# Attention, soft mixture of experts and feed-forward in one kernel: the first pair without conversions, idle transposes and four fold products at the end of attention, one early chunk of w_out

## The chip, the cores and the metric

The kernel runs on one core of a Trainium2 chip. The metric is the device time of one execution in microseconds; where several runs are given, it is their median.

## What is computed

Three stages follow one another. `attn` has 4 batches of 8 heads, 576 positions and 64 dimensions; its result, with the heads side by side, is the input `x` (2304 x 512) of the mixture; the mixture's result is the input of the feed-forward part.

```python
# attention, per head
bias   = -(cumsum(max(s, 0))[i] - cumsum(max(s, 0))[j])
scores = where(causal, -1e9, q @ k.T / 8 + minimum(bias, 0))
x      = softmax(scores) @ v                       # heads side by side: 2304 x 512
# soft mixture of 8 experts with 4 slots each
logits = x @ phi                                   # 2304 x 32
d      = softmax over tokens(logits);  slot_input = d.T @ x
slot_out[e] = maximum(slot_input[e] @ w1[e], 0) @ w2[e]      # 512 -> 1024 -> 512
x      = softmax over slots(logits) @ slot_out
# feed-forward part
h = x @ w_in                                       # 512 -> 2048
g = where(h >= 1, h, where(h <= -1, 0, (h + 1)**2 / 4))
out = g @ w_out                                    # 2048 -> 512
```

`w_in` and `w_out` are 64-bit floats in memory (8 and 8 MB); the kernel reads them as pairs of 32-bit words and makes 32-bit floats of them.

## The kernel before

**Attention** goes over 16 pairs of heads. For each pair TensorE makes the scores (`s_mm`, L267), VectorE the masked minima (`maxima`, L299, recorded at L293), ScalarE the exponentials with their sums (`exps`, L328), TensorE transposes them (L338), ScalarE evacuates the transposes (`evac_p`, L353 and L361), TensorE multiplies by `v` (L369, L377), ScalarE evacuates (L383, L384), and logits (L412) and transposes of the result (L405) follow a pair later. The scores of a pair come in four groups of query blocks; group 2 is the tail of 64 queries of both heads. The bias enters the scores through a second product with the rows `ext`, which come by DMA from `part`, three bfloat16 pieces of the running sum (L222 to L229).

The order of all this is written out by hand: `PLAN` (L52) gives each step a time within its pair of 12 units, `GATE` (L59) does so for the mixture's running softmax of a batch, and the steps are sorted by time and issued. The engines work in the order of issue. All DMAs but two are issued from SP's queue, in order.

Five steps of each pair, W0 to W4, advance `convert_wi` (L581): it loads `w_in` in 32 stages of 256 KB and converts each with one operation on POOL (L601) and two on VectorE (L602, L604). Its first step only starts two stage loads (L590). Each further step issues one half of a stage's work; all of it is done after 65 steps, in the 13th pair. In the plan W1 stands behind the last exponential of group 1 (time 3.9), and M20, the minima of group 2, behind W4 (6.43). The rest of the conversion, `finish_wi` (L608), is 64 operations of VectorE while the experts run.

**The end of attention** (L645 to L677) is the last pair's logits and transposes, then the last batch's gate: `d1` (maximum over blocks), `d2` (transpose and maximum over partitions), `d3` (the maximum is broadcast, `dn` = logits minus maximum; `al4`, the factor for the older sums, as an exponential on ScalarE), `d4` (exponential of `dn`), `c0` to `c2` (the softmax over slots), `d5` (sums, L497, and products with X, L500 and L502, in `pa`), `d6` (running sums). Then the four 32-row groups are folded into one: for each of four blocks of 128 columns one product of the older sum `acc` with `fold_al` (L670) and one of the new part, copied out of PSUM, with `fold` (L671). The result divided by its total is `siT` (L675), which the experts read. `c3` transposes the slot weights into `cstack` (L542, L548, L552).

**The experts** (L691 to L782) run one after the other: `layer1` (L695, then a transpose, L702) and `layer2` (L711, then copy `os` on ScalarE, L714, a transpose, L717, and a copy to `soT`, L718). Their weights come in tiles of 512 KB, four for each `w1` and each `w2`, in the order of `LOADS` (L40). There are 38 places for a tile: 12 `pre` and 10 `post` ones that are filled during attention, 6 more `post` ones and 7 `tmp` ones that exist when the buffers of the heads are free (L649 to L652), and 3 `tmp` ones when all buffers of attention are free (L684). `load_w` (L104) issues loads from SP for as long as there is a free place; a place is given back with the last product that reads it. In the list two chunks of `w_out` (`wo`) stand ahead of the last eight tiles; `wo` may only take a `pre` place. From the third chunk on, the loads of `wo` wait behind a small DMA (`gate`, L126) that reads the last `w2` tile.

Ahead of the last expert's `layer2` the two early chunks are converted to the 32-bit parts `wh` and `wl` (`convert_wo`, L732): one operation on ScalarE (L148), three on VectorE (L150, L152, L154), a cast on ScalarE (L740) and a difference on VectorE (L742).

**The feed-forward part** does not form the mixture's output. It forms M = slot_out @ w_in (`m_part`, L797) once, stacks parts of it (`split_m`, `stack_m`), and then goes over blocks of 384 tokens and 16 blocks of the hidden dimension: `h_part` (product with `cstack`, L830, and two ScalarE activations, L832 and L833), `g_part` (L840 on VectorE, L842 on ScalarE), `l_part` (L848 on VectorE), `o_part` (27 records of products: L858 with `wh`, L859 with `wl`, L860 with `wh`). The first two token blocks alternate, so each chunk of `w_out` is used in two steps running. Chunk n's six conversion steps are spread over the loop's steps from `NWIN * n + CONV_AT` on (L788 to L791).

Of the kernel before, what the change touches and what calls it, by code (L numbers as in the profile page):

```python
# [8 lines left out]
F32 = mybir.dt.float32  # L9
# [3 lines left out]
AF = mybir.ActivationFunctionType  # L13
# [26 lines left out]
LOADS = [(_k, _q) for _k in W_ORDER for _q in range(4)]  # L40
WO_EARLY = 2
WO_SLOTS = 6
LOADS[-8:-8] = [("wo", _q) for _q in range(WO_EARLY)]
LOADS += [("wo", _q) for _q in range(WO_EARLY, 16)]
CHUNK = 256
PRE_FROM, PRE_STEP = (5, 2.4)
NWIN = 2
CONV_AT = -5
CONV_PARTS = 6
# [15 lines left out]
def attention_softmoe_ffn_kernel(  # L65
# [43 lines left out]
    def load_parts():  # L109
        while w_next[0] < len(LOADS):  # L110
            key, q = LOADS[w_next[0]]
            if key == "wo":
                slot = next((f for f in w_free if f[0] == "pre"), None) if len(wo_used) < WO_SLOTS else None
            else:
                slot = w_free[0] if w_free else None
# [4 lines left out]
            if key == "wo":  # L120
                t = t.bitcast(I32)
                wo_used.append(q)
                if q == WO_EARLY:

                    last = w_tiles[W_ORDER[-1]][3][0]
                    nc.sync.dma_start(out=gate[0:1], in_=last[0:1, 0:1])  # L126
                w_wo[q] = t, slot
                src = w_src[key][q // 4][:, 1024 * (q % 4):1024 * (q % 4) + 1024]
            else:
                w_tiles.setdefault(key, []).append((t, slot))  # L130
                src = w_src[key[0]][key[1]][:, 1024 * q:1024 * q + 1024]
# [9 lines left out]

    def convert(src, a, out):

# [3 lines left out]
        ai = a.bitcast(I32)  # L147
        A.activation(out=a, in_=hi.bitcast(F32), func=AF.Copy, scale=2.0 ** -112)  # L148
        yield
# [11 lines left out]
    with att:  # L161
# [55 lines left out]
        for x in ext:  # L217
            G.memset(x, 0.0)
            for h in range(2):
                G.memset(x[64 * h:64 * h + 6, 0], 1.0)  # L220
                G.memset(x[64 * h:64 * h + 6, 1], -1.0)
        V.tensor_scalar(s_sb, s_sb, 0.0, SCALE, op0=ALU.max, op1=ALU.mult)  # L222
# [226 lines left out]
        def gate_parts(b):  # L449
# [19 lines left out]
            def d3():  # L469
# [11 lines left out]
                if b + 1 == B:  # L481
                    rescale()
                if b > 0:
                    st["al4"] = al4 = gt.tile([128, 1], F32, tag="al4", name="al4")
                    A.activation(out=al4, in_=bc[:, 32:33], func=AF.Exp)

            def d4():
                A.activation(out=st["dn"], in_=st["dn"], func=AF.Exp)

            def d5():  # L490
# [131 lines left out]
        for pi in range(NP):  # L622
# [12 lines left out]
            for n, f in dict(LG=logits, XT=x_mm, SL=sc_l, SX=sc_x).items():  # L635
                if pi < NP - 1:
                    step(n, f, pi)
            for k in range(5):
                step(f"W{k}", next, cw, None)
# [15 lines left out]
        parts = gate_parts(B - 1)  # L655
        for n in ("d1", "d2", "d3", "d4", "c0", "c1", "d5", "d6"):
            parts[n]()
        st = parts["st"]
        fold_al = small.tile([128, NSLOT], F32, tag="fa", name="fold_al")
        V.tensor_scalar(fold_al, fold, st["al4"], None, op0=ALU.mult)  # L660
        parts["c2"]()


        tot, sp = bank()[:, 0:32], bank().rearrange("p (c s) -> p c s", c=16)
        T.matmul(out=tot, lhsT=s_run.to_broadcast([128, 128]), rhs=fold, start=True, stop=True)
        new = [ot_p.tile([128, S], F32, tag="ot", name="new") for _ in range(2)]
        A.copy(out=new[0][:, 0:256], in_=st["pa"][:, 0:256])
        V.tensor_copy(new[1][:, 0:256], st["pa"][:, 256:512])
        for c in range(4):
            T.matmul(out=sp[:, c], lhsT=acc[:, 128 * c:128 * c + 128], rhs=fold_al, start=True, stop=False)  # L670
            T.matmul(out=sp[:, c], lhsT=new[c // 2][:, 128 * (c % 2):128 * (c % 2) + 128], rhs=fold, start=False, stop=True)  # L671
        rs = small.tile([128, 1, NSLOT], F32, tag="rs", name="rs")
# [15 lines left out]
    ps_e_ctx = ExitStack()  # L688
    ps_e = ps_e_ctx.enter_context(tc.tile_pool(name="ps_e", bufs=2, space=PSUM))

    def layer1(e, wt):  # L691
# [15 lines left out]
    def layer2(e, wt, hT):  # L707
        p3 = ps_o.tile([128, 128], F32, tag="o0", name="p3")
        for c in range(8):
            for g in range(4):  # L710
                T.matmul(out=p3[32 * g:32 * g + 32, :], lhsT=hT[:, c % 2, c // 2], rhs=wt[c // 2][:, 512 * (c % 2) + 128 * g:512 * (c % 2) + 128 * g + 128],  # L711
                         start=(c == 0), stop=(c == 7))
        os_ = ex.tile([128, 128], F32, tag="os", name="os")
        A.copy(out=os_, in_=p3)  # L714
# [17 lines left out]
    def convert_wo(c):  # L732
# [3 lines left out]
        cv = fin[0].tile([128, 512], F32, tag="cv", name="cv", bufs=4)  # L736
        yield from convert(wt, cv, cv)
        wo_used.remove(c)
        release([slot])
        A.copy(out=wh[c], in_=cv)  # L740
        yield
# [46 lines left out]
    conv = {}  # L788
    for n in range(WO_EARLY, 16):
        for f in range(CONV_PARTS):  # L790
# [81 lines left out]
    def o_next():  # L872
# [5 lines left out]
        done[0] += 1  # L878

    m_part(0, M_A, range(4))  # L880
    split_m(0, M_A)
    h_part(*seq[0])
    h_part(*seq[1])
    m_part(M_A, 512, range(4))
    g_part(*seq[0])
    g_part(*seq[1])
    l_part(*seq[0])
    l_part(*seq[1])
    o_next()
    split_m(M_A, 512)  # L890
# [62 lines left out]
```

## Time and profile before

| | us |
|---|---|
| median of 3 runs | 486.72 |
| lowest, highest of them | 486.53, 491.70 |
| the profiled execution | 486.61 |
| its span, from first to last instruction | 484.6 |
| TensorE busy in it | 456.8 (94%) |
| VectorE, ScalarE, GpSimd busy | 337.0, 334.1, 37.2 |

The profile is of one execution. In a timeline a row gives the start in us from the start of the span, the duration, engine, line, operation, tiles (out<-in), shape, how many instructions were merged, and in brackets how long the engine had been idle before it and what ended that. In windows, a row is a stretch with the busy time of each engine and the number of instructions, the granted clock of TensorE (1.00 is 2.4 GHz, 0.50 is 1.2 GHz), the busy share of the DMA engines and the rate. PE is TensorE, PEld its weight loads, DVE VectorE, ACT ScalarE, POOL GpSimd, SPq SyncE's queue.

### The profile page before, as it was taken

What the parts mean: (1) busy time and instruction counts of PE and PEld (TensorE: products, weight loads), DVE (VectorE), ACT (ScalarE), POOL (GpSimd) and SP (SyncE); (2) the same over time, 40 slices, a digit from 0 to 9 for tenths busy, and PEclk for the clock granted to TensorE, in tenths of its full rate; (3) what the DMA queues carried; (4) which work ended last, traced back from release to release, by engine and by line L of the source; (5) the groups of instructions that cost most, each with busy time, mean ns of one, the idle gap of its engine ahead of it and who ended that gap; (6) DMA issues with size and microseconds to landing.
All of it is one profiled execution on the core that took longest, in us unless ns stands there. A gap on an engine that the chain in (4) does not pass through costs nothing.

```text
span 484.6 us, 11673 instructions
## 1 busy us (share of the span) xinstructions
PE 456.8 (94%) x4394; PEld 334.5 (69%) x4394; DVE 337.0 (70%) x952; ACT 334.1 (69%) x907; POOL 37.2 (8%) x106
## 2 busy tenths in 40 slices
PE   5699999999999997779978999999999999999997
PEld 2476676766676665546644777778888888888885
DVE  6678898888888873599835898896555555555553
ACT  1688897998898896212226888887767677667763
POOL 7111201120220011000000000000000000000000
PEclk9899999999999999589967999999999999999999
DMA  2887867787778316999975820000200100100101
GB/s 65 243 237 203 271 196 209 211 251 225 214 219 231 85 28 231 345 361 410 390 253 208 268 109 0 1 0 27 105 1 0 65 1 0 67 1 17 50 0 65
DMA packets 28425, 71.01 MB, mean 147 GB/s; under 512 B 4018, under 2 KB 5234, under 8 KB 28370
## 3 DMA queue, kind: packets, MB, share of 16 engines
q1 hardware_dynamic: 28358, 70.27, 45.1%
q8 instruction: 34, 0.56, 0.5%
q14 instruction: 21, 0.17, 0.1%
q10 hardware_dynamic: 12, 0.01, 0.0%
HBM read 64.83 MB, written 4.83 MB: 144 GB/s over the span
## 4 chain that ended last, share of the span: by engine, by line
PE 71%; ACT 14%; DVE 5%; issue 4%; DMA 3%; POOL 2%; SPq 1%; ACTq 0%; DVEq 0%; POOLq 0%
PE o L860 14%; PE o L858 13%; PE o L859 13%; ACT P L328 6%; PE s L377 6%; ACT pts L361 5%; PE s L287 4%; PE hp L830 4%; PE s L338 3%; PE p L695 3%; PE s L279 2%; PE s L369 2%; PE p L711 2%; DMA wt<-in_w_dram 2%; PE mp L800 1%
## 5 line engine op out<-in xcount | busy, mean ns | idle before, releaser
L860 PE MATMUL o<-wt,gl 128*128 128x512 f32 x288 | 114.2, 397 | 0.4 <-DVE gl L848 0.4
L858 PE MATMUL o<-wt,gh 128*128 128x512 f32 x288 | 113.3, 393 | 0.1
L859 PE MATMUL o<-wt,gh 128*128 128x512 f32 x288 | 112.8, 392 | 0.0
L328 ACT ACTIVATE P<-s,nm 128x512 f32<-128x512 f32 (+4 forms) x160 | 84.0, 537 | 15.9 <-DVE nm L293 15.7
L842 ACT CAST gh<-g 128x384 fp32r<-128x384 f32 x96 | 49.1, 511 | 51.3 <-DVE g L840 51.1
L293 DVE CUSTOM_DVE_ANT_0 s<-s,tri 128x512 f32<-128x512 f32 (+2 forms) x144 | 68.6, 505 | 20.6 <-ACT pts L361 17.2
L848 DVE TENSOR_TENSOR gl<-g,gh 128x384 fp32r<-128x384 f32 x96 | 53.5, 557 | 38.9 <-ACT gh L842 38.8
L840 DVE SCALAR_TENSOR_TENSOR g<-w,hp 128x384 f32<-128x384 f32 x96 | 53.1, 553 | 38.9 <-ACT w L833 38.9
L860 PEld LDWEIGHTS o<-wt,gl 128*128 128x128 f32 x288 | 54.0, 188 | 16.6 <-DVE gl L848 5.2
L858 PEld LDWEIGHTS o<-wt,gh 128*128 128x128 f32 x288 | 54.3, 188 | 12.7 <-issue 0.7
L279 PE MATMUL s<-x 64*128 64x512 f32 (+3 forms) x256 | 54.1, 472 | 7.8 <-DMA x<-in_qkT_dram 5.0
L859 PEld LDWEIGHTS o<-wt,gh 128*128 128x128 f32 x288 | 54.3, 189 | 8.2
L832 ACT ACTIVATE w<-hp,half 128x384 f32<-128x384 f32 x96 | 55.3, 576 | 1.1 <-PE hp L830 1.1
L833 ACT ACTIVATE w<-w 128x384 f32<-128x384 f32 x96 | 50.4, 525 | 3.0
L361 ACT COPY pts<-s 128x512 f32<-128x512 f32 (+3 forms) x128 | 47.3, 454 | 1.2
L338 PE MATMUL s<-ident,P 64*128 64x64 f32 x800 | 38.7, 230 | 2.8 <-ACT P L328 2.6
L279 PEld LDWEIGHTS s<-x 64*128 64x128 f32 x256 | 27.2, 196 | 15.9 <-DMA x<-in_qkT_dram 5.6
L338 PEld LDWEIGHTS s<-ident,P 64*128 64x128 f32 x800 | 32.4, 140 | 7.7 <-ACT P L328 3.2
L377 PE MATMUL s<-pts,v 128*64 128x512 f32 (+3 forms) x256 | 37.3, 433 | 0.0
L328 ACT ACTIVATION_READ_ACCUMULATOR P<-s,nm 128x1 f32 x160 | 34.7, 217 | 0.0
L830 PE MATMUL hp<-cstack,mst 96*128 96x384 f32 x96 | 32.9, 346 | 1.7 <-DVE mst L810 1.0
L377 PEld LDWEIGHTS s<-pts,v 128*64 128x64 f32 x256 | 17.3, 137 | 17.0 <-issue 14.4
(145 smaller groups left out, 577.9 us busy)
## 6 DMA issues: line engine op xcount, KB each, us to landing
wt<-in_w_dram SPq DMA_DIRECT2D x64, 512.0 KB
x<-in_qkT_dram SPq DMA_DIRECT2D x32, 288.0 KB
st<-in_w_in_dram SPq DMA_DIRECT2D x32, 256.0 KB
wt<-in_w_out_dram SPq DMA_DIRECT2D x16, 512.0 KB
out_dram<-ob SPq DMA_DIRECT2D x18, 256.0 KB
v<-in_v_main_dram SPq DMA_DIRECT2D x16, 256.0 KB
ext<-exts SPq DMA_DIRECT2D x60, 3.4 KB
v<-in_v_tail_dram SPq DMA_DIRECT2D x16, 32.0 KB
```

The lines of the kernel that those rows point to most:

```text
L279: T.matmul(out=o[h][:, off:off + n], lhsT=y[r, 0, c:c + 128], rhs=y[r, 1, 0:n], start=(k == 0), stop=(k == 1))
L293: V.tensor_tensor_reduce(out=sc, in0=sc, in1=mask[:, mask.shape[1] - n:], scale=-1.0 / SCALE, scalar=init, op0=ALU.add, op1=ALU.min, accum ...
L328: A.activation(out=out_, in_=in_, func=AF.Exp, bias=nm, scale=-1.0, accum_out=sm[:, k:k + 1])
L338: T.transpose(out=o[f][:, c:c + 64], in_=P[r], identity=ident[r, r])
L361: A.copy(out=d, in_=i.rearrange("p h (j q) -> p h j q", q=64))
L377: T.matmul(out=o[r, 128 * j:512], lhsT=vt[:, j, r], rhs=pts_t[pi][:, h, 512 * j:384 * j + 512], start=(j == 0), stop=(j == 3))
L832: A.activation(out=w, in_=hp, func=AF.Relu, bias=half, scale=0.5)
L840: V.scalar_tensor_tensor(out=g, in0=w, scalar=1.0, in1=hp, op0=ALU.min, op1=ALU.max)
L848: V.tensor_tensor(out=gl, in0=g, in1=gh.bitcast(F32), op=ALU.subtract)
L858: T.matmul(out=o_t[j][t], lhsT=gh[:, r], rhs=wh[c], start=(c == 0), stop=False)
L859: T.matmul(out=o_t[j][t], lhsT=gh[:, r], rhs=wl[c], start=False, stop=False)
L860: T.matmul(out=o_t[j][t], lhsT=gl[:, r], rhs=wh[c], start=False, stop=(c == 15))
```

## The change

- In pair 0 only W0 is issued; the steps of `convert_wi` slide to later pairs.
- In the setup the rows of ones and minus ones in `ext` are written by ScalarE activations from `ones` instead of by POOL memsets.
- At the end of attention 22 transposes of the identity into a bank that nobody reads (`warm`) are issued between the steps d1 to d4. The exponential `al4` of the last batch goes behind the exponential of `dn`. The order of `c2` and `d6` is turned round. The older sum is scaled and added to the new part on VectorE, so that four fold products are left instead of eight.
- One chunk of `w_out` instead of two is loaded early, directly ahead of the last `w2`, and it may take a `post` place. The second is loaded right behind the last `w2`, the gate stands ahead of the third, and the second's conversion runs at the start of the feed-forward part with POOL in place of ScalarE.
- In the last `layer2` one idle transpose is issued behind each of the first three tiles.
- The other chunks' conversions start one step later.

```diff
-WO_EARLY = 2
+WO_EARLY = 1
+WO_FIRST = 2
 WO_SLOTS = 6
-LOADS[-8:-8] = [("wo", _q) for _q in range(WO_EARLY)]
+WARM_E = 1
+LOADS[-4:-4] = [("wo", _q) for _q in range(WO_EARLY)]
 LOADS += [("wo", _q) for _q in range(WO_EARLY, 16)]
+WI_0 = (0,)
+WARM_T = (9, 4, 2, 3, 4)
-CONV_AT = -5
+CONV_AT = -4
...
-                slot = next((f for f in w_free if f[0] == "pre"), None) if len(wo_used) < WO_SLOTS else None
+                slot = next((f for f in w_free if f[0] == "pre" or q < WO_EARLY and f[0] == "post"), None) if len(wo_used) < WO_SLOTS else None
...
-                if q == WO_EARLY:
+                if q == WO_FIRST:
...
-        A.activation(out=a, in_=hi.bitcast(F32), func=AF.Copy, scale=2.0 ** -112)
+        if pool:
+            G.tensor_scalar(a, hi.bitcast(F32), 2.0 ** -112, 1.0, op0=ALU.mult, op1=ALU.mult)
+        else:
+            A.activation(out=a, in_=hi.bitcast(F32), func=AF.Copy, scale=2.0 ** -112)
...
         for x in ext:
             G.memset(x, 0.0)
+        for x in ext:
             for h in range(2):
-                G.memset(x[64 * h:64 * h + 6, 0], 1.0)
-                G.memset(x[64 * h:64 * h + 6, 1], -1.0)
+                for a in range(2):
+                    A.activation(out=x[64 * h:64 * h + 6, a], in_=ones[0:6], func=AF.Copy, scale=1.0 - 2.0 * a)
...
-                if b > 0:
+                st["bc"] = bc
+                if b + 1 < B:
+                    exp_al()
+
+            def exp_al():
+                if b > 0:
                     st["al4"] = al4 = gt.tile([128, 1], F32, tag="al4", name="al4")
-                    A.activation(out=al4, in_=bc[:, 32:33], func=AF.Exp)
+                    A.activation(out=al4, in_=st["bc"][:, 32:33], func=AF.Exp)

             def d4():
                 A.activation(out=st["dn"], in_=st["dn"], func=AF.Exp)
+                if b + 1 == B:
+                    exp_al()
...
-            for k in range(5):
+            for k in range(5) if pi else WI_0:
                 step(f"W{k}", next, cw, None)
...
-        for n in ("d1", "d2", "d3", "d4", "c0", "c1", "d5", "d6"):
+        idle = bank()
+        def warm(n):
+            for _ in range(n):
+                T.transpose(out=idle[:, 0:128], in_=ident, identity=ident)
+        for n, k in zip(("d1", "d2", "d3", "d4"), WARM_T):
+            warm(k)
+            parts[n]()
+        warm(WARM_T[4])
+        for n in ("c0", "c1", "d5", "c2"):
             parts[n]()
         st = parts["st"]
-        fold_al = small.tile([128, NSLOT], F32, tag="fa", name="fold_al")
-        V.tensor_scalar(fold_al, fold, st["al4"], None, op0=ALU.mult)
-        parts["c2"]()
+        parts["d6"]()
...
-        A.copy(out=new[0][:, 0:256], in_=st["pa"][:, 0:256])
-        V.tensor_copy(new[1][:, 0:256], st["pa"][:, 256:512])
+        for i in range(2):
+            V.scalar_tensor_tensor(out=new[i][:, 0:256], in0=acc[:, 256 * i:256 * i + 256], scalar=st["al4"],
+                                   in1=st["pa"][:, 256 * i:256 * i + 256], op0=ALU.mult, op1=ALU.add)
         for c in range(4):
-            T.matmul(out=sp[:, c], lhsT=acc[:, 128 * c:128 * c + 128], rhs=fold_al, start=True, stop=False)
-            T.matmul(out=sp[:, c], lhsT=new[c // 2][:, 128 * (c % 2):128 * (c % 2) + 128], rhs=fold, start=False, stop=True)
+            T.matmul(out=sp[:, c], lhsT=new[c // 2][:, 128 * (c % 2):128 * (c % 2) + 128], rhs=fold, start=True, stop=True)
...
+            if e + 1 == NE and c % 2 and c < 7:
+                warm(WARM_E)
...
-        yield from convert(wt, cv, cv)
+        yield from convert(wt, cv, cv, c == WO_EARLY)
...
-        A.copy(out=wh[c], in_=cv)
+        if c == WO_EARLY:
+            G.tensor_copy(wh[c], cv)
+        else:
+            A.copy(out=wh[c], in_=cv)
...
-    for n in range(WO_EARLY, 16):
+    for n in range(WO_EARLY + 1, 16):
...
+    one_c = gens[WO_EARLY]
+    next(one_c)
     m_part(0, M_A, range(4))
     split_m(0, M_A)
+    next(one_c)
+    next(one_c)
+    next(one_c)
     h_part(*seq[0])
     h_part(*seq[1])
     m_part(M_A, 512, range(4))
     g_part(*seq[0])
     g_part(*seq[1])
+    next(one_c)
     l_part(*seq[0])
     l_part(*seq[1])
+    next(one_c, None)
     o_next()
```

## Rows read from the trace of the kernel before

**Rows 1.** The page's strip of the granted clock, 40 slices of 12.1 us.

```profile
PEclk9899999999999999589967999999999999999999
```

**Rows 2.** The timeline of the first pair and the start of the second.

```profile
4.66 1.04 DVE L225 CAST part<-cum 32x576 bf16<-32x576 f32 x1
...
6.52 0.53 DVE L225 CAST part<-cum 32x576 bf16<-32x576 f32 x1
...
16.07 1.07 ACT L361 COPY pts<-s 128x512 f32<-128x512 f32 x2
...
18.54 0.29 DVE L602 TENSOR_SCALAR st<-st 128x256 int32<-128x256 int32 x1 [3.42 <-DMA st<-in_w_in_dram]
...
19.48 0.46 DVE L293 CUSTOM_DVE_ANT_0 s<-s,tri 128x288 f32<-128x288 f32 x1
...
20.76 0.50 ACT L328 ACTIVATE P<-s,nm 128x288 f32<-128x288 f32 x1 [3.62 <-DVE nm L293]
...
25.53 0.67 ACT L361 COPY pts<-s 128x256 f32<-128x256 f32 x2
...
31.16 0.52 ACT L328 ACTIVATE P<-s,nm 128x288 f32<-128x288 f32 x1
...
35.87 0.67 ACT L361 COPY pts<-s 128x256 f32<-128x256 f32 x2
```

**Rows 3.** Windows: a stretch of pair 13.

```profile
165.00:175.00 10.00, 10.00 (x141) 6.46 (x139) 7.66 (x32) 7.51 (x25) 0.78 (x3) 1.00 0.11 31
```

**Rows 4.** The timeline of the end of attention, and single transposes among the experts.

```profile
194.71 0.27 PE L458 MATMUL s<-ident,mx 128*32 128x128 f32 x1 [1.51 <-DVE mx L454]
...
204.48 21.51 SPq L133 DMA_DIRECT2D wt<-in_w_dram  x21
...
206.01 3.49 PE L695 MATMUL p<-wt,siT 128*32 128x256 f32 x32 [0.51 <-ACT cstack L552]
...
226.06 0.44 PE L702 MATMUL p<-ident,hs 128*128 128x128 f32 x2
...
228.29 0.33 PE L717 MATMUL p<-ident,os 128*128 128x128 f32 x1
```

**Rows 5.** Windows around the clock's fall; the first with L338's transposes alone.

```profile
185.00:187.70 2.70, 1.44 (x32) 1.24 (x32) 1.00 0.87 262
...
193.20:195.80 2.60, 0.44 (x4) 0.29 (x3) 1.84 (x8) 2.15 (x10) 0.00 (x0) 0.95 0.96 310
195.80:206.00 10.20, 8.77 (x59) 5.91 (x59) 5.22 (x18) 1.68 (x6) 0.32 (x1) 0.50 0.93 347
```

**Rows 6.** Windows of the weight stream; the last column is GB/s.

```profile
204.00:208.00 4.00, 3.49 (x27) 1.92 (x30) 3.46 (x7) 0.69 (x2) 0.00 (x0) 0.50 0.70 230
...
232.00:242.00 10.00, 10.00 (x216) 6.61 (x208) 8.61 (x17) 2.24 (x9) 0.00 (x0) 1.00 1.02 388
242.00:247.00 5.00, 3.44 (x91) 2.46 (x94) 0.89 (x2) 1.60 (x5) 0.00 (x0) 0.98 1.02 395
```

**Rows 7.** The waits of SP's queue: total us, times, longest.

```profile
SPq L133 <- PE p L695: 8.4, 6, 5.4
```

**Rows 8.** The timeline of the last expert's end and of M.

```profile
249.54 1.08 PE L711 MATMUL p<-wt,hT 128*32 128x128 f32 x16 [0.46 <-DMA wt<-in_w_dram]
...
251.29 0.26 ACT L714 COPY os<-p 128x128 f32<-128x128 f32 x1
...
252.34 1.93 PE L800 MATMUL mp<-wif,soT 128*32 128x128 f32 x32 [0.26 <-ACT soT L718]
...
256.19 4.85 PE L800 MATMUL mp<-wif,soT 128*32 128x384 f32 x32
```

**Rows 9.** The timeline of the feed-forward loop's first steps.

```profile
266.46 0.45 PE L830 MATMUL hp<-cstack,mst 96*128 96x384 f32 x1 [0.71 <-DVE g L840]
...
268.54 0.69 DVE L742 TENSOR_TENSOR wt<-cv,wt 128x512 fp32r<-128x512 f32 x1
...
272.83 0.40 PE L859 MATMUL o<-wt,gh 128*128 128x512 f32 x1
```

More of the change, by code (lines that the diff above doesn't have):

```diff
@@ L140, in evac, with convert @@
             V.tensor_copy(out, in_)
-    def convert(src, a, out):
+    def convert(src, a, out, pool=False):
         w = src.rearrange("p (n two) -> p n two", two=2)
@@ L689, in attention_softmoe_ffn_kernel, with warm @@
     ps_e = ps_e_ctx.enter_context(tc.tile_pool(name="ps_e", bufs=2, space=PSUM))
+    idle_t = []
+    def warm(n):
+        for _ in range(n):
+            if not idle_t:
+                idle_t.append(ps_e.tile([128, 128], F32, tag="e", name="idle"))
+            T.transpose(out=idle_t[0], in_=ident, identity=ident)
     def layer1(e, wt):
```

## The prediction, made before the change was run

> **What bounds the kernel now.** I read the page first, and in it the strip of the granted clock [rows 1]. The reader is to see four low places in it: slice 2 (the first pair of heads), slices 16 and 17 (the end of attention into the first expert) and slices 20 and 21 (the last expert into the feed-forward part). They are where TensorE had been idle, and they are the places that the change touches. Elsewhere TensorE is busy 9 tenths of each slice, and nothing in the diff touches its work there. Then I read the timeline around each place, the windows of the stretches between them, and the waits of SP's queue.
>
> Three stretches have three different limits. In the first pair VectorE stands still: L602, the first conversion of `w_in`, waits 3.42 us for its DMA, and the minima of the tail block (L293) are queued behind it; ScalarE's exponentials then wait 3.62 us for them [rows 2]. From pair 1 on TensorE and ScalarE set the pace. From the end of attention to the last expert the weight stream is the limit: the DMA engines are busy all the time at some 395 GB/s [rows 6], and the last tiles of the last `w2` arrive after the engines want them [rows 8].
>
> **Part 1: the first pair.** Only the two stage loads of W0 stay in pair 0; two conversions leave it. VectorE had finished its last minimum at 18.54 - 3.42 = 15.12. The two minima of the tail block take 20.76 - 19.48 = 1.28 to the first exponential, so they would be ready at 16.4 instead of 20.7. What is late next is ScalarE: it evacuates transposes until 16.07 + 1.07 = 17.14 [rows 2]. The exponentials then start at 17.2 instead of 20.76: **3.5 us**. The low clock there adds no more: from these exponentials to the last evacuation of the pair it is 26.20 - 20.76 = 5.44 at the low clock and 36.54 - 31.16 = 5.38 a pair later [rows 2]. Bounds: 0, if another wait takes its place, and 3.6.
>
> In the setup POOL's eight small memsets become eight ScalarE activations from `ones`. VectorE's first cast of `part` took 1.04 beside POOL's wide memset and the next one 0.53 [rows 2]; POOL will be through its wide memsets by then, and the first `ext` DMAs follow `part` directly. I take **0.5** gained. Nearest row for an activation of this width: the 128x288 ones at 0.50 [rows 2], so some 0.6 to 0.8 each for 576 elements, 5 to 6.4 us in all plus a table load before 8.4, when `part` is ready. At the long end ScalarE issues its two `ext` DMAs late by 0.7. Bounds: 0.9 gained, 0.7 lost.
>
> The steps of `convert_wi` slide by a pair: they end in pair 13 instead of 12, so two of them (about 1.4 us of VectorE) now stand in pair 13. There VectorE was busy 7.66 of 10 us and TensorE all of it [rows 3]; TensorE's work hides them. I charge **0.1**; 0.5 if the cover is thin.
>
> **Part 2: the end of attention.** Four of the eight fold products go; two scaled sums on VectorE come in place of two copies; 22 idle transposes come in between. One transpose is 0.33 and two are 0.44 [rows 4], so 0.11 for each further one at full clock, twice that at half. At full clock thirteen of them are 1.4 us in front of the transpose of the maxima, which waits 1.51 there [rows 4]: hidden. Seven more stand in front of the sums, 0.8 us; the `al` exponential, moved behind the `dn` one on ScalarE, gives about half of that back. From 195.8 to 206.0 TensorE was busy for 8.77 us at clock 0.50 [rows 5]; at full clock that is 4.4. With 0.6 back for the seven transposes and for the two sums, which stand in the chain, the first expert would start at 206.0 - 4.4 + 0.6 = 202.2 [rows 4]. If the clock falls anyway, only the four products are saved, less some slow transposes: about 1 us.
>
> This gain is not the kernel's. The experts behind it are limited by the weight stream, so only two things count. First, SP waits for the last fold product before it can issue the next loads: its next issue is at 204.48 [rows 4], and in 204 to 208 the engines move 230 GB/s instead of 395 [rows 6]. (395 - 230) x 4 / 395 = 1.7 us of the stream are lost. With the folds done by 201 the loads are issued before the earlier ones run dry, and the hole closes: **1.7** (0.8 if the clock falls in spite of the transposes, 0 if the rate does not come back).
>
> Does the idle work hold the clock? In 185.0 to 187.7 TensorE was busy for 1.44 us in transposes and hardly anything else, and the clock stayed full; in 193.2 to 195.8 it was busy for 0.44 us and the clock fell at the end of it [rows 5]. With the idle transposes TensorE does in the second stretch what it did in the first, so I expect full clock.
> The Trainium skill (TensorE: Matmul & The Clock Gate, Part 4: PE-mode transpose) says that work in transpose mode does not count as TensorE activity in the way that matmuls do, so the clock would fall as before. The row of 185 us speaks against it but not strictly, since matmuls stand on both sides; by that rule the result would be rival 2 below.
>
> **Part 3: one chunk of w_out ahead.** One chunk of 512 KB fewer stands ahead of the last `w2`: 0.524 MB / 395 GB/s = **1.3 us** earlier (0 to 1.5). The order also changes which slots are asked for: SP waited up to 5.4 us for a `pre` slot [rows 7], and around it, in 232 to 242, the rate was 388 against 395 behind it [rows 6]; now the first chunk may take a `post` slot, of which some are free by then. (395 - 388) x 10 / 395 = **0.2** (0 to 0.5). The second chunk is loaded behind the last `w2` without the gate; it is later in the same queue, so I charge nothing (up to 0.5 if the two share the engines).
>
> The last group of the last expert, which started on its DMA at 249.54 [rows 8], so starts 1.7 + 1.3 + 0.2 = 3.2 earlier. Behind it ScalarE's copy `os` stood at 251.29 behind the cast of the second chunk, and the feed-forward part's first product M began at 252.34. That is 1.7 us after the group's end (249.54 + 1.08 = 250.62); copy 0.26, transpose 0.48, copy 0.17 and the hops make 1.05 without the cast. **0.7** gained.
>
> **Part 4: the start of the feed-forward part.** Chunk 1 is now converted here: POOL first (waits for its DMA, with nothing behind it), then three VectorE operations of 1.8 us in a hole in which VectorE waits 1.95 for ScalarE; 0, or 0.3 lost. Later chunks start one step later. That takes about 1.1 us of VectorE and one ScalarE conversion from in front of the first `g` of the loop, for which TensorE waited 0.71 [rows 9]: **0.7** gained (0 to 1.5, the total of the small holes there). The price is slack: the low part of chunk 2 was ready at 268.54 + 0.69 = 269.23 and first used at 272.83 [rows 9], 3.6 us; one step (2.35) later leaves 1.2. It still holds.
>
> What of the clock here? Three idle transposes in the last expert are 0.3 us of filling, while each group of 0.5 us now waits some 1.3 for its tile, from an earlier point on than before, because the engines arrive sooner. I expect the clock to fall again, and M to run at half clock as before (1.93 and 4.85 [rows 8]).
>
> **The sum.** 3.5 + 0.5 - 0.1 + 1.7 + 1.3 + 0.2 + 0.7 + 0.7 = 8.5, from the profiled execution's 486.6 (span 484.6 and 2.0 around it): **478.1 us**. The median of the runs shown is 486.72, 0.1 above, so nothing is corrected.
>
> **Rivals.**
> 1. The clock holds, or is back, through M. For it: the three transposes, and the groups themselves get longer when the clock is low. Against it: the longer waits. M's two parts would take some 1.0 and 2.6 instead of 1.93 and 4.85, about 3.1 us less: 475.0. Chance 0.18.
> 2. The transposes do not hold the clock at the end of attention (half clock from 195.8, folds done at 203.4). The hole then closes by 0.8 instead of 1.7, 0.9 less gained: 479.0; with the hole not closing at all, 479.8. Chance 0.17.
> 3. The first pair gains almost nothing: the exponentials wait for something else that comes late, such as the banks of the second pair or its `x`. For it: the early DMAs run at 80% of the engines' time. Against it: ScalarE's own queue is the only thing that ended after 16.4. 3.5 less gained: 481.6. Chance 0.09.
> 4. Slower: the conversions, one step later, become late. The low part of a chunk (L742) is last in VectorE's heavier step; if it ends more than 1.2 us later than I place it, TensorE waits at the second product of each of the 14 chunks. With 0.8 us for each that is 11.2, and 478.1 + 11.2 = 489.3; from 0.6 us for each on (8.5 / 14) the change is no gain. Against it: the slack of 3.6 is measured, and the step 2.35. Chance 0.04.
>
> **How the numbers follow.** The forecast, with each part as taken, has 0.52, and its own range is 476.5 to 479.7 (the 0.5 and 0.7 terms at either bound). The range of 473.8 to 481.8 takes in rivals 1 to 3 with their bounds and leaves out rival 4 and the far ends. One per cent, 4.9 us, is about what a measurement tells from no change: below 481.8 are the forecast, rivals 1 and 2 and most of rival 3. Faster 0.9, same 0.07, slower 0.03.
>
> **What would show it.** Right: in the first pair no VectorE wait on `st`, and the first exponential of the tail block near 17; clock 1.00 from the last pair to the first expert; 390 GB/s without a hole from there on; the last expert's last group near 242 (249.5 - 3.9 - 3.2), no cast ahead of `os`; M at 1.9 and 4.9. Wrong: exponentials in pair 0 still past 19; the stream with a new hole; TensorE waiting for L742 or for POOL's cast; pairs 13 longer by more than half a microsecond.

## The result, and the profile after

| | before | changed |
|---|---|---|
| median, us | 487.58 (4 runs) | 475.25 (4 runs) |
| lowest, highest | 486.53, 491.70 | 474.67, 475.83 |
| ratio, 95% interval | | 0.973 (0.967 to 0.979) |
| the profiled execution, its span | 486.61, 484.6 | 475.83, 474.1 |

The change is faster by 2.7%. The forecast was 478.1, 1.8% below the 486.7 of before; its range holds the measured time. The same kernel taken a second time (control `c1` below) gave 477.24, ratio 0.977 (0.974 to 0.981): faster too, but by an interval that reaches past 2%. The size of the change is somewhere between the two.

The strip of the granted clock, from the page of the changed kernel, against [rows 1]:

```profile
PEclk9999999999999999999959999999999999999999
```

The low places of the first pair and of the end of attention are gone. One is left, in slice 20 (counted from 0; by this count the first pair's low place before was slice 1): the end of the last expert and M.

The timeline of the first pair, changed kernel (columns as in [rows 2]):

```profile
4.50 0.51 DVE L233 CAST part<-cum 32x576 bf16<-32x576 f32 x1
...
11.58 0.70 DVE L301 CUSTOM_DVE_ANT_0 s<-s,tri 128x512 f32<-128x512 f32 x1 [2.66 <-PE s L287]
...
15.44 0.53 DVE L301 CUSTOM_DVE_ANT_0 s<-s,tri,nm 128x288 f32<-128x288 f32 x1 [0.15 <-DVE nm L301]
...
15.82 1.07 ACT L369 COPY pts<-s 128x512 f32<-128x512 f32 x2
16.76 0.53 ACT L336 ACTIVATE P<-s,nm 128x288 f32<-128x288 f32 x1
```

VectorE goes through its minima with a gap of 0.15 where it had stood for 3.42. The first exponential of the tail block (L336) follows ScalarE's own copies at 16.76, with no wait in brackets; before it was 20.76.

The timeline of the end of attention, TensorE alone, against [rows 4]:

```profile
188.44 1.64 PE L676 MATMUL s<-ident 128*128 128x128 f32 x13
190.02 0.27 PE L466 MATMUL s<-ident,mx 128*32 128x128 f32 x1
...
191.89 0.98 PE L676 MATMUL s<-ident 128*128 128x128 f32 x7
...
195.15 1.08 PE L695 MATMUL s<-fold,new 128*128 128x32 f32 x8
...
197.46 1.93 PE L727 MATMUL p<-wt,siT 128*32 128x256 f32 x32 [0.59 <-ACT cstack L567]
```

L676 are the idle transposes. The first 13 fill the wait in front of L466. Each of the four fold products (L695) has two records here. The first expert (L727) starts at 197.46 instead of 206.01, and its 32 products take 1.93 instead of 3.49: full clock.

Windows of the weight stream in the changed kernel (the last three columns are clock, DMA share and GB/s), against [rows 5, 6]:

```profile
180.00:195.00 15.00, 12.15 (x173) 8.53 (x167) 7.53 (x31) 7.91 (x31) 1.60 (x5) 1.00 0.96 324
195.00:208.00 13.00, 9.89 (x190) 6.64 (x193) 12.16 (x26) 2.64 (x8) 0.00 (x0) 1.00 1.03 410
208.00:222.00 14.00, 13.05 (x288) 8.52 (x281) 13.35 (x26) 3.30 (x11) 0.00 (x0) 1.00 1.03 408
222.00:232.00 10.00, 9.76 (x207) 6.11 (x199) 9.52 (x19) 2.17 (x8) 0.00 (x0) 1.00 1.03 407
232.00:239.00 7.00, 4.94 (x104) 3.14 (x104) 2.60 (x5) 2.38 (x6) 0.00 (x0) 1.00 1.03 408
```

There is no hole: some 408 GB/s from 195 on. Before had one window of 230, in 204 to 208, and behind it, ahead of its 388 and 395:

```profile
208.00:222.00 14.00, 10.67 (x214) 6.32 (x206) 13.33 (x26) 2.74 (x9) 0.00 (x0) 0.96 1.01 391
222.00:232.00 10.00, 9.92 (x223) 6.86 (x227) 9.59 (x18) 2.51 (x9) 0.00 (x0) 1.00 1.02 406
```

So the rate of the changed kernel is nothing new; what is new is that it holds throughout.

The timeline of the last expert's end and of M, all engines, against [rows 8]:

```profile
237.12 0.64 PE L743 MATMUL p<-wt,hT 128*32 128x128 f32 x16 [1.62 <-DMA wt<-in_w_dram]
...
238.31 0.65 PE L743 MATMUL p<-wt,hT 128*32 128x128 f32 x16 [0.29 <-DMA wt<-in_w_dram]
...
239.59 1.08 PE L743 MATMUL p<-wt,hT 128*32 128x128 f32 x16 [0.38 <-DMA wt<-in_w_dram]
...
241.01 1.08 PE L743 MATMUL p<-wt,hT 128*32 128x128 f32 x16
...
242.22 0.27 ACT L748 COPY os<-p 128x128 f32<-128x128 f32 x1 [3.46 <-PE p L743]
...
243.27 1.93 PE L837 MATMUL mp<-wif,soT 128*32 128x128 f32 x32 [0.26 <-ACT soT L752]
...
247.12 3.95 PE L837 MATMUL mp<-wif,soT 128*32 128x384 f32 x32
```

TensorE arrives early and waits 1.62 for the first tile; the next two groups start on their DMAs 1.2 and 1.3 later. One tile, 0.524 MB at 408 GB/s, is 1.28. The first two groups take 0.64 and 0.65, the third and the fourth 1.08: the clock falls between them. `os` (L748) comes 0.13 behind the last group (241.01 + 1.08 = 242.09), with no cast ahead of it. M starts at half clock, as forecast, but it gets the full clock back before its second part ends (3.95 instead of 4.85).

To follow the sum, I cut the span at four marks (all in us from its start): the first product with `v` of pair 15 (P15), the start of the last expert's last group, M's start, and the first output product O.

| stretch, us | before | forecast change | changed | `c1` |
|---|---|---|---|---|
| start to P15 | 188.87 | -3.9 | 184.18 | 184.51 |
| P15 to last group | 60.67 | -3.2 | 56.83 | 57.50 |
| last group to M | 2.80 | -0.7 | 2.26 | 2.26 |
| M to O | 8.63 | 0 | 7.73 | 9.14 |
| O to end | 223.63 | -0.7 | 223.10 | 223.09 |
| span | 484.6 | -8.5 | 474.1 (-10.5) | 476.5 (-8.1) |

### The profile page after: what moved, and what is told of

It is laid out like the page before. It is cut to its first block, busy times and chain, and to the rows that moved or that the text cites. A ratio compares the mean times of both kernels' runs of the same rounds, so it can differ in the third digit from the quotient of the medians.

```text
span 474.1 us, 11728 instructions
## 1 busy us (share of the span) xinstructions
PE 451.4 (95%) x4411; PEld 331.4 (70%) x4411; DVE 336.7 (71%) x952; ACT 338.2 (71%) x912; POOL 34.7 (7%) x100
## 4 chain that ended last, share of the span: by engine, by line
PE 68%; ACT 16%; DMA 8%; DVE 5%; issue 2%; SPq 0%; ACTq 0%; DVEq 0%
PE o L897 14%; PE o L895 13%; PE o L896 13%; ACT P L336 7%; DMA wt<-in_w_dram 7%; PE s L385 6%; ACT pts L369 5%; PE s L295 4%; PE hp L867 4%; PE s L346 3%; PE s L287 2%; PE s L377 2%; PE mp L837 1%; PE p L743 1%; DVE s L301 1%
## 5 line engine op out<-in xcount | busy, mean ns | idle before, releaser
L336 ACT ACTIVATE P<-s,nm 128x512 f32<-128x512 f32 (+4 forms) x160 | 84.4, 544 | 16.0 <-DVE nm L301 15.7
L287 PE MATMUL s<-x 64*128 64x512 f32 (+3 forms) x256 | 52.4, 463 | 5.0 <-DMA x<-in_qkT_dram 5.0
L336 ACT ACTIVATION_READ_ACCUMULATOR P<-s,nm 128x1 f32 x160 | 35.7, 223 | 0.0
L287 PEld LDWEIGHTS s<-x 64*128 64x128 f32 x256 | 26.2, 192 | 13.0 <-DMA x<-in_qkT_dram 5.8
```

The lines of the kernel that those rows point to most:

```text
L287: T.matmul(out=o[h][:, off:off + n], lhsT=y[r, 0, c:c + 128], rhs=y[r, 1, 0:n], start=(k == 0), stop=(k == 1))
L336: A.activation(out=out_, in_=in_, func=AF.Exp, bias=nm, scale=-1.0, accum_out=sm[:, k:k + 1])
```

## Experiments

The first four kernels ran beside runs of before with a median of 488.22, `c1`, `e8`, `e5`, `e6` beside 487.47, the last three beside 487.16. Times of the same kernel differ by several us here, so each verdict goes by the marks first.

**e1: the conversions back in pair 0.**

```diff
-WI_0 = (0,)
+WI_0 = range(5)
```

> The changed kernel with the conversions of w_in back in the first pair. Theory (VectorE's wait for the first stage of w_in is what the first pair lost): the first exponential of the tail block stands near 20.5 us instead of 16.76, TensorE's clock falls in slice 2 again, and the whole is 4.0 to 4.7 us longer, 479.5 to 480. Rival (the gain came from the setup, the stall was hidden behind ScalarE anyway): at most 0.7 longer.

478.69 us, ratio 0.981 (0.976 to 0.985). The wait is back in the timeline of this kernel:

```profile
17.34 0.30 DVE L617 TENSOR_SCALAR st<-st 128x256 int32<-128x256 int32 x1 [2.48 <-DMA st<-in_w_in_dram]
...
19.56 0.50 ACT L336 ACTIVATE P<-s,nm 128x288 f32<-128x288 f32 x1 [2.68 <-DVE nm L301]
```

The exponentials are 2.8 later than in the changed kernel, the first product with `v` of pair 0 3.5 (26.08 against 22.58), P15 4.0, the last group 4.2. I expected the exponentials 3.7 later; the other 1.2 to before's 20.76 go with the old setup, which before has as well. The time is 3.4 above the changed kernel's first measurement and 1.5 above the control. So what is lost in the first pair reaches the end of the experts in this trace; from M to O, 6.96, part of it is paid back. In this execution the last pair's products with `v` ran at half clock as well (3.80 against 2.32); no run tells why.

**e2: no idle transposes at the end of attention.**

```diff
-WARM_T = (9, 4, 2, 3, 4)
+WARM_T = (0, 0, 0, 0, 0)
```

> The changed kernel without the 22 idle transposes at the end of attention; four fold products and the new order stay. Theory (the transposes hold the clock): the granted clock falls to 0.50 some 7 us before the first expert, the first expert starts 1.5 to 3 us later than 197.46, a hole comes back into the weight stream, and the last tile's group of the last expert is 0.5 to 1.2 later; the whole 0.5 to 1.5 longer, less if the clock is then full in M. Rival (transposes do not count for the clock, by the skill's page; it held for another reason): the clock stays 1.00, the first expert starts 0 to 0.5 earlier, the whole within 0.3.

477.26 us, ratio 0.977 (0.973 to 0.982). The windows, and then the timeline of the last expert and M (TensorE alone):

```profile
190.00:195.00 5.00, 3.93 (x38) 1.69 (x38) 3.48 (x14) 1.19 (x5) 0.32 (x1) 0.59 0.91 303
195.00:200.00 5.00, 4.45 (x27) 3.17 (x30) 3.74 (x10) 0.69 (x2) 0.00 (x0) 0.50 1.02 379
```

```profile
240.08 0.65 PE L743 MATMUL p<-wt,hT 128*32 128x128 f32 x16 [0.52 <-ACT hT L736]
...
242.58 0.65 PE L743 MATMUL p<-wt,hT 128*32 128x128 f32 x16
...
244.26 1.08 PE L837 MATMUL mp<-wif,soT 128*32 128x128 f32 x32 [0.26 <-ACT soT L752]
...
246.87 2.79 PE L837 MATMUL mp<-wif,soT 128*32 128x384 f32 x32
```

Without the transposes the clock falls to 0.50 in the tail, and `e9` below repeats that, so they do hold it up to the first expert. The Trainium skill (TensorE: Matmul & The Clock Gate, Part 4: PE-mode transpose) says that transposes do not count as TensorE activity in the way that matmuls do; here the clock was 1.00 with them and 0.50 without, which is not what that rule would give. From P15 to the first expert it is 17.14 before, 15.00 here, 13.28 in the changed kernel: the fewer products and the new order gave 2.1, and the transposes with the clock that they hold 1.7 (I expected 1.5 to 3 for these). And yet the total is the control's, 2.0 above the changed kernel's first measurement. The engines reach the last expert later, find its tiles landed (the group waits for ScalarE, not for a DMA), keep the full clock, and get back in M what they lost: M to O is 5.33 here. The `gate`, which waits for the last `w2` tile, was issued at 241.12, and at 240.82 in the changed kernel. That is less than the 1.0 by which this mark differs between two executions of the changed kernel (241.82 in `c1`), so in this trace no loss of the stream can be told. Of O to end (225.41 here) about 1.0 is one wait at 331 behind a store of the output.

**e4: two chunks ahead again.** The old place in `LOADS`, `pre` places only, and chunk 1 converted as before:

```diff
-WO_EARLY = 1
+WO_EARLY = 2
...
-LOADS[-4:-4] = [("wo", _q) for _q in range(WO_EARLY)]
+LOADS[-8:-8] = [("wo", _q) for _q in range(WO_EARLY)]
...
-    one_c = gens[WO_EARLY]
-    next(one_c)
...
```

> The changed kernel with two chunks of w_out ahead of the last two w2 again, both converted ahead of the last expert's second layer on ScalarE and VectorE, none at the start of the feed-forward part. Theory (each chunk ahead costs its place in the stream, and the second cast holds os up): the last group of the last expert starts 1.3 to 1.7 later than 241.01, M 1.9 to 2.4 later than 243.27, the whole 1.7 to 2.4 longer, 477 to 477.7. Rival (the stream was shortened by the closed hole and the faster rate, the chunk is hidden): within 0.5.

478.3 us, ratio 0.980 (0.975 to 0.986). The cast is back ahead of `os` (ScalarE's timeline):

```profile
243.63 0.62 ACT L774 CAST wt<-cv 128x512 fp32r<-128x512 f32 x1 [2.01 <-DVE cv L161]
244.16 0.26 ACT L748 COPY os<-p 128x128 f32<-128x128 f32 x1
```

From the last group's end (242.53) to M (245.06) it is 2.53 against 1.18: the cast costs 1.35 here, not 0.7. The last group itself is 0.9 later than in the changed kernel (I expected 1.3 to 1.7) and level with the control, and by time the kernel is 3.1 above the one and 1.1 above the other: in the right direction, in size between 1 and 3.

**e7: many idle transposes in the last expert.**

```diff
-WARM_E = 1
+WARM_E = 5
...
+        if e + 1 == NE:
+            warm(14)
```

> The changed kernel with 14 idle transposes ahead of the last expert's second layer and 5 instead of 1 behind each of its first three tiles. Theory (the clock falls at 239.6 because TensorE waits for the last tiles, and idle transposes hold it): clock 1.00 through M, whose parts take some 1.0 and 2.6 instead of 1.93 and 3.95; the whole 1.5 to 2.8 shorter, 472.5 to 473.8. Rival (transposes do not hold the clock there, or they stand in front of the groups): clock 0.50 in M as now, the whole the same or up to 1 longer.

475.07 us, ratio 0.972 (0.967 to 0.977); I expected 472.5 to 473.8. M runs at 1.08 and 2.79, but the last group starts at 242.89, 1.9 later than in the changed kernel. TensorE's timeline, and windows of the experts before it:

```profile
237.18 0.44 PE L734 MATMUL p<-ident,hs 128*128 128x128 f32 x2
237.46 1.69 PE L721 MATMUL idle<-ident 128*128 128x128 f32 x14
239.08 0.65 PE L745 MATMUL p<-wt,hT 128*32 128x128 f32 x16
239.65 0.77 PE L721 MATMUL idle<-ident 128*128 128x128 f32 x5
240.35 0.64 PE L745 MATMUL p<-wt,hT 128*32 128x128 f32 x16
```

```profile
195.00:200.00 5.00, 4.41 (x45) 2.55 (x45) 4.50 (x11) 0.69 (x2) 0.00 (x0) 0.78 1.02 414
200.00:205.00 5.00, 3.92 (x70) 3.00 (x66) 4.76 (x10) 0.76 (x2) 0.00 (x0) 0.54 1.03 408
```

The groups stand 1.27 apart, no more than in the changed kernel (3.89 for three steps there), so the five transposes behind each did not make the delay; the first group is 1.96 late already. In this execution the clock fell just behind the first expert's start, although the idle transposes of the tail were there, and TensorE reached the last second layer 2.1 later (L734 at 237.18 against 235.05). The fourteen transposes then stood in front of the first group. All tiles had landed by 241.00, where the `gate` was issued; with 0.84 from group to group, as in `e2`, part of the delay could have been caught up, and the five transposes prevented that. The clock in M is worth having; what this many transposes cost with the experts on time, this run does not show.

**c1: the changed kernel once more,** as a control.

> The changed kernel as it is, on the chip and in the rounds of the next three. Theory (the change is worth some 10.5 us in its stages, and the clock's falls after the first expert come at different places in different executions): 474.5 to 476 us, first expert near 197.5, last group of the last expert between 241 and 243. Rival (the profiled execution was a lucky one): 477 or more.

477.24 us (six runs, 474.21 to 478.33), ratio 0.977 (0.974 to 0.981). That lies in the rival's range: the first measurement, 475.25, was on the lucky side. TensorE's timeline:

```profile
244.27 1.94 PE L837 MATMUL mp<-wif,soT 128*32 128x128 f32 x32 [0.26 <-ACT soT L752]
...
248.13 5.35 PE L837 MATMUL mp<-wif,soT 128*32 128x384 f32 x32
```

Here M is at half clock from end to end, and M to O is 9.14 instead of 7.73. Executions of one kernel differ by where the clock comes back. That is 1.4 of the 2.4 between the two spans; the `gate`, 1.0 later here, makes up most of the rest. By the mean clocks on record, the slowest three runs of `c1` (477.6 to 478.3) had 0.985 and 0.986, the next two (475.65 and 476.89) 0.989, and the fastest (474.21) 0.996. The four runs of the first measurement show no such order.

**e8: idle transposes in step with the stream.** Twelve fill the wait for the first tile, three stand behind each of the first three groups.

```diff
-WARM_E = 1
+WARM_E = 3
...
+        if e + 1 == NE:
+            warm(12)
```

> The changed kernel with 12 idle transposes ahead of the last expert's second layer and 3 instead of 1 behind each of its first three tiles, so that they fit between two tiles of the stream. Theory (with 5 each the groups stood 1.27 us apart behind their own transposes; with 3 the stream sets their pace and the clock holds): last group by 241.5, M's parts 1.1 and 2.8, first output product near 248.5, 472.3 to 473.8 us. Rival (the clock's fall is not in our hands there): M at half clock, as the changed kernel within 0.5.

474.1 us, ratio 0.972 (0.969 to 0.975), 0.3 above the range that I expected; six runs from 473.28 to 474.18, each below every one of the control's on the same chip. The timeline, TensorE:

```profile
236.11 1.47 PE L721 MATMUL idle<-ident 128*128 128x128 f32 x12
237.51 0.65 PE L745 MATMUL p<-wt,hT 128*32 128x128 f32 x16
238.09 0.55 PE L721 MATMUL idle<-ident 128*128 128x128 f32 x3
...
240.66 0.65 PE L745 MATMUL p<-wt,hT 128*32 128x128 f32 x16
...
242.34 1.08 PE L839 MATMUL mp<-wif,soT 128*32 128x128 f32 x32 [0.26 <-ACT soT L754]
...
244.95 2.79 PE L839 MATMUL mp<-wif,soT 128*32 128x384 f32 x32
```

The last group starts as early as in the changed kernel, M to O is 5.32, and the span is 471.5. O to end is 0.7 longer than there (223.84), so a part is paid back in the loop. This is the version that beats both kernels, and its runs lie within 0.9 us. In this execution, too, the clock fell behind the first expert's start (0.77 in 195 to 200; the first expert's 32 products took 3.21), and TensorE reached the last second layer 0.8 later than in the changed kernel, so its wait there was shorter as well. That the transposes alone keep M at full clock rests on the six times more than on this one trace.

**e5: the setup's memsets back on POOL.**

```diff
-        for x in ext:
...
-                for a in range(2):
-                    A.activation(out=x[64 * h:64 * h + 6, a], in_=ones[0:6], func=AF.Copy, scale=1.0 - 2.0 * a)
+                G.memset(x[64 * h:64 * h + 6, 0], 1.0)
+                G.memset(x[64 * h:64 * h + 6, 1], -1.0)
```

> The changed kernel with the ones and minus ones of ext written by POOL memsets again. Theory (VectorE's first cast of part is slowed by POOL's wide memset, and the first products with ext follow part): the first minimum 0.2 to 0.3 later than 11.58, the first cast near 1.0 again, and the whole 0.2 to 0.6 longer, as no later wait absorbs it. Rival (the first pair's DMAs set the pace): no difference.

476.6 us, ratio 0.977 (0.974 to 0.979), no different from the control. The marks say more. Timeline, VectorE:

```profile
4.66 1.05 DVE L232 CAST part<-cum 32x576 bf16<-32x576 f32 x1
...
12.33 0.70 DVE L300 CUSTOM_DVE_ANT_0 s<-s,tri 128x512 f32<-128x512 f32 x1 [1.67 <-PE s L286]
```

The first cast, beside POOL's wide memset (4.34 to 5.40), takes 1.05 instead of 0.51. The Trainium skill (GPSIMD Engine Reference, 8. Key points) says that GpSimd shares its SBUF interfaces with VectorE, so that it contends with VectorE instructions that have two SBUF inputs or use a two-port mode; the slower cast fits, but no row tells whether it is such an instruction. The first minimum is 0.75 later, three times what I expected, and P15 1.0. (In before, with the same memsets, the first minimum stands at 11.83, so this mark alone differs by 0.5 between two kernels with the same setup.) The loss does not reach the time in this kernel: in the profiled execution the groups of the last expert ran at 1.08 early on, the clock was back for M (1.08 and 2.79), and that hid it.

**e6: conversions one step earlier.**

```diff
-CONV_AT = -4
+CONV_AT = -5
```

> The changed kernel with the conversions of the later chunks one step earlier, as before. Theory (conversions in front of g at the loop's start held TensorE up): from the first output product to the end 0.5 to 1.0 longer than 223.1, with a wait of TensorE for g in the third step, whole 0.4 to 1.0 longer. Rival (the loop's first steps are limited by ScalarE and the split of M, wherever the conversions stand): within 0.2.

476.43 us, ratio 0.976 (0.974 to 0.979): not to be told from the control by time. But the wait of [rows 9] is back:

```profile
256.75 0.44 PE L867 MATMUL hp<-cstack,mst 96*128 96x384 f32 x1 [0.70 <-DVE g L877]
...
260.98 0.50 PE L897 MATMUL o<-wt,gl 128*128 128x512 f32 x1 [0.42 <-DVE gl L885]
```

and O to end is 224.24 against 223.10: the later conversions are worth 1.1.

**e9: e8 without the transposes of attention's end.** It asks what those are worth when M keeps its clock in any case.

```diff
-WARM_T = (9, 4, 2, 3, 4)
+WARM_T = (0, 0, 0, 0, 0)
```

> The kernel of e8 (idle transposes on pace in the last expert) without the 22 transposes at the end of attention. Theory (with the clock held at the end, the experts' own chain counts again: without the tail's transposes it starts some 1.4 us later and at half clock): first expert near 198.8, last group 1 to 2 later than 240.66, clock full in M, the whole 0.8 to 2 longer than e8, 475 to 476. Rival (the weight stream alone sets the end of the experts): within 0.4 of e8.

475.18 us, ratio 0.975 (0.972 to 0.978), 1.1 above `e8`. Its windows show the half clock:

```profile
195.00:200.00 5.00, 4.45 (x31) 3.30 (x27) 3.38 (x9) 0.69 (x2) 0.00 (x0) 0.50 1.03 384
```

The first expert starts 2.3 later than in `e8`, the last group 2.2. The marks agree with the price, and the time shows half of it. The stream is set back as well, unlike in `e2`:

```profile
200.00:205.00 5.00, 3.90 (x46) 1.63 (x42) 4.80 (x10) 0.76 (x2) 0.00 (x0) 0.67 0.97 355
```

`e8` has 413 in this window, and its `gate` is issued at 240.45, that of `e9` at 242.42.

**b1: the kernel before with the transposes of e8.** The same `warm(12)` and `warm(3)` put into `layer2` of before.

> The kernel before with the same 12 and 3 idle transposes in its last expert and nothing else of the change. Theory (half clock in M is a loss of its own, independent of the parts of the change): M's parts 1.1 and 2.8 instead of 1.93 and 4.85; os still behind the second chunk's cast; the whole 2 to 3.5 shorter than before, 484 to 485.5. Rival (the cast and the conversions on ScalarE set that stretch, the clock does not matter): within 0.7 of before.

485.94 us, ratio 0.997 (0.994 to 1.000): 1.2 between the medians, less than I expected. The groups and M's first part are at full clock, but `os` still stands behind the cast of the second chunk, TensorE waits 1.30 for it, and the clock falls once more: TensorE's timeline has 1.08 for M's first part at 252.66, but 1.01 instead of 0.62 for the `h` products at 254.72. By this one trace, the transposes need the freed ScalarE beside them.

**e3: no idle transposes in the last expert.**

```diff
-WARM_E = 1
+WARM_E = 0
```

> The changed kernel without its three idle transposes in the last expert. Theory (three are too few to hold the clock, which falls there with them too): same as the changed kernel within its own spread, 475 to 478. Rival (they shorten the time at half clock): 1 or more longer than the changed kernel, 478 to 479.5.

476.1 us, ratio 0.976 (0.973 to 0.979), M at 1.94 and 5.35, as in the control. The change's own three transposes do nothing that can be measured.

## Why the prediction was right, and where it was not

Right in kind: the forecast of faster, the places, and that M would start at half clock. By the marks the two profiled executions give 10.5 and 8.1 where 8.5 stood; the measured medians give 12.3 and 10.2 against their own runs of before, which were 0.8 to 0.9 above the forecast's base. So the forecast was too small. (Its own range of 476.5 to 479.7 does not follow from the bounds that it names: 0.4 and 0.8 down give 476.9, 1.2 and 0.7 up give 480.0.)

- **The first pair and the setup.** The first exponential of the tail block moved by 4.0, which is 3.5 + 0.5 as worked out; ScalarE's own copies set it, as said. Taken back one at a time, the conversions cost 2.8 (`e1`) and the setup 0.75 (`e5`) at this mark; the remaining 0.45 shows only with both. The step that failed is "the low clock there adds no more". I had compared a pair at the low clock with one at full clock, 5.44 against 5.38, but the second had a wait of its own (0.32 of ScalarE for VectorE at 34.58) where the first had one for TensorE (0.38 at 24.89), and the stretch ended at ScalarE's last evacuation, ahead of the products with `v`. From the exponential to the first product with `v` it is 6.38 before (mean clock 0.91 in 9 to 27) and 5.82 after (1.00). `e8` and `e9`, the same there but for the clock that was granted, have 5.83 and 6.44. So the clock is 0.6, and P15 came 4.7 earlier instead of 3.9. Eight activations took 5.09, 0.64 each, inside the estimate.
- **Pair 13.** Pair 0 to P15 is 161.60 against 161.73: the charge of 0.1 was nothing.
- **The end of attention.** The first expert starts 3.86 earlier counted from P15, forecast 3.8. The parts are open: the fewer products and the new order gave 2.1 (`e2`), the transposes and the clock 1.7. The forecast had "about 1 us" for a fallen clock, but with slow transposes in it, and `e2` has none, so the two figures are not of the same thing. The transposes were priced a little low: thirteen took 1.64 and seven 0.98, where 1.4 and 0.8 were taken at 0.11 each, without the 0.33 of the first in a row.
- **"This gain is not the kernel's."** The hole closed, and with the one chunk less and the places the last group came 3.84 earlier counted from P15 (3.17 in `c1`), forecast 3.2. For the stream alone a better mark is the time from P15 to the `gate`, by which the last tile has landed. It is 60.64 before and 60.77 in `b1`. In the eight executions that have the idle transposes of the tail and one early chunk (the changed kernel, `c1`, `e1`, `e3`, `e5` to `e8`) it is 56.55 to 57.31, 57.0 in the mean. So the stream ends 3.7 earlier, and the eight spread by 0.8. Without the tail's transposes it is 57.29 (`e2`, inside the eight) and 58.29 (`e9`, 1.0 outside). So the tail's clock can cost the stream up to 1.3, but most of the hole closes without it: SP issues its next loads 15.6 after P15 before, 12.1 in the changed kernel, 13.4 in `e2` and 13.8 in `e9`. That the clock closes the hole was the wrong reason; the fewer products with the new order do most of it, and the changed places may have a part that no run separates. The limit of 395 GB/s was wrong as well: before itself had 406 in 222 to 232.
- **One chunk.** With two chunks ahead (`e4`) the `gate` is at 57.72 from P15, 0.8 above the mean of the eight and 0.4 above the highest. So the chunk is worth about 0.8, where 1.3 was taken, and one execution stands behind that. For the cast `e4` gives 1.35, where 0.7 was taken; in the changed kernel only 0.54 of it show, since before's cast was less late.
- **M.** Half clock as forecast, but 4.85 was taken as if it were fixed: 3.95 and 5.35 were seen in two executions. Rival 1's mechanism is real (1.08 and 2.79, against 1.94 and 5.35, are 3.4; I had 3.1), but neither profiled execution of the changed kernel has it. `e5`, with the same last expert, has it, so some executions of the changed kernel may. That the median of 475.25 is close to rival 1's 475.0 is luck: it came by other terms.
- **The loop.** 0.5 from O to the end, 1.1 by `e6`; 0.7 was taken.
- **The rivals.** Rival 2 falls with the windows after (1.00) and `e2` (0.50); rival 3 with the first pair's rows. Rival 4 did not come: from the first output product to 285 one row of TensorE's products has a wait, and it is for `gl`:

```profile
261.84 0.50 PE L897 MATMUL o<-wt,gl 128*128 128x512 f32 x1 [0.20 <-DVE gl L885]
```

What stays open: why the clock falls in the first pair of some executions and not of others of like code (`e9` against `e8`), why it fell behind the first expert's start in `e7` and `e8` and not in the changed kernel, and at what moment it comes back in M.

## What to carry to other kernels

Where a transfer sets the pace, engines that arrive earlier only wait, and the wait can cost more than it saved, because the work behind it starts at half clock: in `e2` TensorE came to the last expert's groups later than in the changed kernel, did not wait there for a tile, and reached O at 249.59, against 251.00 and 253.41. Look at what stands behind the last wait before paying for an earlier arrival. Idle transposes are a cheap way to bridge such a wait (0.11 us for each behind the first), if they are as many as fit between two tiles: one behind each tile changed nothing that could be measured (`e3`), and more than fit stand in front of work that is ready, as the fourteen in `e7` do. Where the time of one kernel spreads by several us, compare marks in the trace of each run, and cut the span into stretches that add up.

## What was not expected of the hardware

- Executions of one kernel took 474.2 to 478.3 us. In the two that were profiled, the largest difference in one stretch is the clock's, M to O at 7.73 or 9.14. With the waits filled (`e8`) the spread of the times was 0.9.
- The idle transposes of attention's end held the clock at 1.00 up to the first expert in eight traces (in a ninth, `e1`, it had fallen ahead of them), but in two of the eight, `e7` and `e8`, it fell to 0.50 just behind the first expert's start.
- A slower stretch can be paid back in full by the clock behind it: against the control `e2` loses 1.7 from P15 to the first expert and gains 3.8 from M to O.
- The weight stream ran at 408 GB/s from 195 to 239 in the changed kernel, where I had taken 395 as its limit; before came near it in one window (406).
